# The head of a fused attention and expert kernel: key rows, query casts and the order of the first tiles

## The chip, the cores and the metric

The kernel runs on one core of one Trainium2 chip. The metric is the device time of one execution in microseconds (us); lower is better. TensorE is called PE, VectorE DVE, ScalarE ACT, GpSimd POOL and SyncE SP, as in the profile.

## The reference

Attention with pooled keys and values feeds a mixture of four experts:

```python
k_p = k.reshape(B, H, Sp, 8, D).mean(axis=3)        # B 8, H 8, S 576, D 64, Sp 72
v_p = v.reshape(B, H, Sp, 8, D).mean(axis=3)
attn = softmax(q @ k_p^T / sqrt(D))                 # 576 x 72 per head
x = (attn @ v_p) as (B*S, H*D)                      # 4608 x 512
p = domain_probs / (domain_probs.sum(-1) + 1e-9)
out = sum over e of p[:, e] * (relu(x @ w1[e]) @ w2[e])   # w1 512x1024, w2 1024x512, 4 experts
```

All inputs and the output are float32 in DRAM.

## The kernel before, in words

**Tiling.** The 4608 tokens are 36 tiles of 128 (`t`), four to a group of 512 (9 groups). For each tile the kernel makes the scores of 8 heads against 72 pooled keys (`scores`, line 381), subtracts the row maximum (`less_max`, 392), takes the exponential (`expo`, 405), turns the result (`turn_e`, 438) and multiplies with the pooled values (`context`, 458, or `context_turned`, 487). Queries have to be turned so that the head dimension lies on the partitions (`turn_q`, 352): for early tiles PE transposes rows of bf16 queries (`qrow`) into PSUM and ACT copies them out; for tiles from `DT` = 11 on DVE transposes 32x32 blocks of a block-wise loaded batch (`qblk`), with no work for PE. The experts are steps `s` (9 groups x 4 experts) of eight `up` products (503) and four `down` products (534), each of 128x512 outputs; `collect` (546) adds the weighted result and stores a tile after the last expert.

**Order.** The program is written out by hand (`manual_schedule`, 71): each engine executes its instructions in the order in which the code emits them. After the head, a loop over steps and slots (697) emits one `up` or `down` per slot and, from a plan with slots (571 to 611), the attention work of later tiles. A load by POOL converts float32 to bf16 on its way. It takes one of eight semaphores in turn, so each waits, on POOL, for the landing of the eighth before it.

**The loads at the start.** SP loads the first batch's keys as float32 in three parts (rows 0 to 1, 2 to 3, and the last 64 rows, 148), with the queries of tiles 0 and 1 (`q01`, float32, 512 KB) between the second part and the last (159 to 161). Then come the domain probabilities. POOL prepares masks, then waits in `after` (187, called in 191) for the second key part, by copying one element of it, and from there issues loads: values of batch 0, w1 of expert 0 with `q23` (queries of tiles 2 and 3 as bf16) between its halves, w2 of expert 0, and so on up to w2 of expert 3 and the queries of tile 9 (192 to 212).

**The head** (624 to 695) is a straight list. DVE folds the pooled keys (`fold`, 267; `last_k`, 275), PE transposes them (`turn_k`, 292), ACT casts the queries of tiles 0 and 1, and the first four tiles go through attention one after another, with the first expert's products for single tiles (`up_tile`, 515) between. `warm(n)` (615) issues n products of zeros on PE, of which nothing is used. The queries of tile 2 are turned in line 652, behind `context(0)` and `divide(0)`:

```python
    context(0)
    divide(0)
    turn_q(2)
    warm(5)
    turn_x(0, copy_v)
    turn_e(1)
    turn_q(3)
    scores(2)
```

Of the kernel before, what the change touches and what calls it, by code (L numbers as in the profile page):

```python
# [10 lines left out]
ALU = mybir.AluOpType  # L11
# [6 lines left out]
def kernel(  # L18
# [26 lines left out]
    ROWS = H * SP  # L45
    NB = 5
    TAIL = ROWS - (NB - 1) * P
    DT = 2 * TPG + 3
    EXP_SCALE = 1.0 / (float(D) ** 0.5 * POOL)
    NZ = 4  # L50
    BLK = 32
# [5 lines left out]
    raw = ctx.enter_context(tc.tile_pool(name="raw", bufs=1))  # L57
    prep = ctx.enter_context(tc.tile_pool(name="prep", bufs=2))
    qpool = ctx.enter_context(tc.tile_pool(name="qpool", bufs=8))
    qbpool = ctx.enter_context(tc.tile_pool(name="qbpool", bufs=2))  # L60
    soft = ctx.enter_context(tc.tile_pool(name="soft", bufs=2))
    grp = ctx.enter_context(tc.tile_pool(name="grp", bufs=2))
# [18 lines left out]
    def rows_of(src):  # L81
        return src.rearrange("h (j r) d -> (h j) (r d)", r=POOL)

    def load_rows(eng, dst, rows, parts=((0, NB - 1), (NB - 1, NB))):
        for i0, i1 in parts:
            if i1 == NB:
                src, to = rows[i0 * P:ROWS], dst[0:TAIL, i0, :]
            else:
                src = rows[i0 * P:i1 * P].rearrange("(i p) x -> p i x", p=P)
                to = dst[:, i0:i1, :]  # L90
            eng.dma_start(out=to, in_=src)  # L91

    def load_k(b):
        load_rows(nc.gpsimd, kraw[b % 2], rows_of(k[b]))
# [17 lines left out]
    def load_q(t):  # L112
        qrow[t] = qpool.tile([P, NPAIR, 2, D], BF16, name="qrow")
        for b, tok, n, at in segments(t * P, P):
            for z in range(2):
                nc.gpsimd.dma_start(
                    out=qrow[t][at:at + n, :, z, :],
                    in_=q[b][z * NPAIR:(z + 1) * NPAIR, tok:tok + n, :].rearrange(
                        "c p d -> p c d"
                    ),  # L120
                )
# [12 lines left out]
    def load_w1(e, halves=(0, 1)):  # L134
        for half in halves:
            cols = slice(half * (F // 2), (half + 1) * (F // 2))
            nc.gpsimd.dma_start(
                out=w1_sb[e][:, :, cols],
                in_=moe_w1[e].rearrange("(kc p) f -> p kc f", p=P)[:, :, cols],
            )  # L140
# [3 lines left out]
            out=w2_sb[e][:], in_=moe_w2[e].rearrange("(fb p) d -> p fb d", p=P)  # L144
        )


    KPARTS = ((0, 2), (2, NB - 1), (NB - 1, NB))
    k0 = raw.tile([P, NB, POOL * D], F32, name="k0")
    q01 = raw.tile([P, H, 2, D], F32, name="q01")  # L150
    q23 = raw.tile([P, H, 2, D], BF16, name="q23")

    def load_qg(eng, dst, c):
        eng.dma_start(
            out=dst[:],
            in_=q[0][:, 0:G, :].rearrange("h (p c) d -> p h c d", c=TPG)[:, :, c:c + 2],
        )

    load_rows(nc.sync, k0, rows_of(k[0]), KPARTS[:2])
    load_qg(nc.sync, q01, 0)  # L160
    load_rows(nc.sync, k0, rows_of(k[0]), KPARTS[2:])
    dp0 = const.tile([P, TPG, E], F32, name="dp0")
    nc.sync.dma_start(
        out=dp0[:], in_=moe_domain_probs[0:G].rearrange("(p c) e -> p c e", c=TPG)
# [22 lines left out]
    def after(landed):  # L187

        nc.gpsimd.tensor_copy(out=gate[:], in_=landed)

    after(k0[0:1, NB - 2, POOL * D - 1:POOL * D])
    load_v(0)
    load_w1(0, (0,))
    load_qg(nc.gpsimd, q23, 2)
    load_w1(0, (1,))
    load_w2(0)
    load_w1(1)
    ident32 = const.tile([NL, NL], F32, name="ident32")
# [10 lines left out]
    load_w1(3)  # L209
    load_q(TPG + 4)  # L210
    load_w2(3)
    load_q(TPG + 5)

    vblks = [raw.tile([P, NB, NZ, D], BF16, name=f"vblk{i}") for i in range(2)]
    nc.scalar.memzero(vraw[0][TAIL:P, NB - 1, :])
# [14 lines left out]
    mask_v = const.tile([P, NB, MZ, D], BF16, name="mask_v")  # L230

    def spread_mask():
        nc.vector.tensor_copy(
            out=mask_v[:], in_=own[:, :, 1:NZ].unsqueeze(3).to_broadcast([P, NB, MZ, D])
        )

# [30 lines left out]
    def fold(rows, i0, i1, *widths):  # L267
        for n in widths:
            w = n * D
            nc.vector.tensor_add(  # L270
                out=rows[:, i0:i1, 0:w], in0=rows[:, i0:i1, 0:w],
                in1=rows[:, i0:i1, w:2 * w],
            )

    def last_k(b, rows, i0, i1, n=P):

        if i0 == 0:
            pads[b] = prep.tile([P, NB, 2, D], BF16, name="kpad")
        shape = [n, i1 - i0, 2, D]
        nc.vector.tensor_add(  # L280
            out=pads[b][0:n, i0:i1],
            in0=rows[0:n, i0:i1, 0:D].unsqueeze(2).to_broadcast(shape),
            in1=rows[0:n, i0:i1, D:2 * D].unsqueeze(2).to_broadcast(shape),
        )
# [60 lines left out]
    def turned(dst, blocks, nm, copy=None):  # L345
        n = len(blocks)
        ps = ps_t.tile([P, n, P], BF16, tag="t", name=f"{nm}_ps")
        for i, block in enumerate(blocks):
            nc.tensor.transpose(ps[:, i, :], block, ident[:])  # L349
        (copy or nc.scalar.copy)(out=dst, in_=ps[:])  # L350

    def turn_q(t, copy=None):
        qT[t] = soft.tile([P, NPAIR, P], BF16, name="qT")
        if t >= DT:
            for b, tok, n, at in segments(t * P, P):
                nc.vector.transpose(  # L356
                    out=qT[t][:, :, at:at + n],
                    in_=qblk[b][:].rearrange("p (c a) j -> p c (a j)", c=NPAIR)[
                        :, :, tok:tok + n
                    ],  # L360
                )
            return
        if 2 <= t < TPG:
            ps = ps_t.tile([P, NPAIR, P], BF16, tag="t", name="qT_ps")
            for h in range(H):
                z, c = divmod(h, NPAIR)
                nc.tensor.transpose(
                    ps[z * D:(z + 1) * D, c, :], q23[:, h, t - 2, :], ident[:]
                )
            (copy or nc.scalar.copy)(out=qT[t][:], in_=ps[:])  # L370
            return
        if t < 2:
            qrow[t] = qpool.tile([P, NPAIR, 2, D], BF16, name="qrow")
            nc.scalar.copy(
                out=qrow[t][:],
                in_=q01[:, :, t, :].rearrange("p (z c) d -> p c z d", z=2),
            )
        flat = qrow[t][:].rearrange("p c z d -> p (c z d)")
        turned(qT[t][:], [flat[:, i * P:(i + 1) * P] for i in range(NPAIR)], "qT", copy)

    def scores(t):
        sc = ps_s.tile([P, 2, 512], F32, name="sc")
# [55 lines left out]
    def turn_e(t, copy=None):  # L438
        eT[t] = soft.tile([P, NB, P], BF16, name="eT")
        e = ebuf[t % 2]  # L440
        turned(eT[t][:], [e[:, i * P:(i + 1) * P] for i in range(NB)], "eT", copy)
# [14 lines left out]
    xps = {}  # L456

    def context(t):
        xps[t] = ps = ps_t.tile([P, DM], F32, tag="t", name="x_ps")
        for b, _, n, at in segments(t * P, P):  # L460
            for c, (i, z0, z1) in enumerate(CHUNKS):
                nc.tensor.matmul(  # L462
                    ps[at:at + n, (2 * i - 2 + z0) * D:(2 * i - 2 + z1) * D],
                    lhsT=eT[t][:, i, at:at + n],
                    rhs=vblk[b][:, i, z0:z1].rearrange("p z d -> p (z d)"),
                    start=(c == 0), stop=(c == NB - 1),
                )

    def divide(t):
        rows_x[t] = soft.tile([P, H, D], BF16, name="xr")  # L470
        nc.vector.tensor_tensor(
            out=rows_x[t][:], in0=xps.pop(t)[:].rearrange("p (h d) -> p h d", d=D),
            in1=es.pop(t)[:].unsqueeze(2).to_broadcast([P, H, D]), op=ALU.mult,
        )

    def x_columns(t):
        g, col = t // TPG, (t % TPG) * P
# [4 lines left out]
    def turn_x(t, copy=None):  # L482
        flat = rows_x.pop(t)[:].rearrange("p h d -> p (h d)")
        dst = x_columns(t)
        turned(dst, [flat[:, i * P:(i + 1) * P] for i in range(KC)], "xT", copy)

    def context_turned(t):
        ps = ps_t.tile([P, KC, P], F32, tag="t", name="xT_ps")
# [126 lines left out]
    def warm(n):  # L615

        ps = ps_h.tile([P, 2 * P], F32, tag="h", name="warm_ps")
        for _ in range(n):
            nc.tensor.matmul(ps[:], lhsT=zero[:, 0:P], rhs=zero[:])

    def copy_v(out, in_):
        nc.vector.tensor_copy(out=out, in_=in_)  # L622

    fold(k0, 0, 2, 4, 2)
    last_k(0, k0, 0, 2)
    fold(k0, 2, 4, 4, 2)
    last_k(0, k0, 2, 4)
    spread_mask()
    fold(k0[0:TAIL], 4, 5, 4, 2)
    last_k(0, k0, 4, 5, TAIL)  # L630
    warm(34)
    turn_k(0, copy_v, (
        lambda: None, lambda: None, lambda: None,
        lambda: (warm(12), turn_q(0), warm(2)),
    ))
    warm(3)
    scores(0)
    turn_q(1)
    less_max(0)
    expo(0)  # L640
    warm(10)
    scores(1)
    less_max(1)
    sum_v_by_products(0)
    turn_e(0)
    expo(1)
    spread_v(0)
    warm(5)
    sums_by_products(0)
    context(0)  # L650
    divide(0)
    turn_q(2)
    warm(5)
    turn_x(0, copy_v)
    turn_e(1)
    turn_q(3)
    scores(2)
    less_max(2)
# [3 lines left out]
    context(1)  # L662
    divide(1)
    turn_e(2)
    turn_x(1, copy_v)
    scores(3)
    less_max(3)
    up_tile(0, 1, (0,))
# [1 line left out]
    sums_by_products(2)  # L670
    context(2)
    divide(2)
    up_tile(0, 0, (1,))
    up_tile(0, 1, (1,))
    turn_x(2, copy_v)
    turn_e(3)
    domain_first()
    up_tile(0, 2, (0,))
# [10 lines left out]
    down(0, 2)  # L689
    collect(0, 2)  # L690
    load_k(2)
    load_v(2)
    load_q(TPG + 6)
    load_qblk(2)
    load_qblk(3)

    for s in range(NSTEP):
# [41 lines left out]
```

## Time and profile before

| what | us |
|---|---|
| median of 3 runs | 565.67 (565.13 to 566.07) |
| the profiled execution | 566.62 |
| its span, first to last instruction | 564.9 |
| PE busy, DVE, ACT, POOL | 553.8, 275.1, 251.9, 70.7 |
| granted clock of PE, mean | 0.999 |
| PE first at the turn of tile 2's queries | 17.61 |
| PE first at the dense products of step 1 (L509) | 37.51 |

The profile is of one execution. Its page gives the busy time of each engine, the span in 40 slices with the busy share of each in tenths, the transfer queues, the chain of work that ended last, and the costliest groups. Views of the trace give the instructions in order of time: start, duration, engine, line of the code, operation, output <- input, and in brackets how long the engine had been idle and what ended that. A line number is that of kernel.py and can be a helper's: L349 is the transpose in `turned`, whatever tile it works on. Matmuls overlap, so a group's duration is longer than its share of the chain.

### The profile page before, as it was taken

How to read it: one execution, taken by the hardware profiler on the slowest of the kernel's cores; microseconds unless marked ns; L12 is line 12 of the kernel's file. 1: busy time of each engine (PE TensorE's matmuls, PEld its weight loads, DVE VectorE, ACT ScalarE, POOL GpSimd, SP SyncE). 2: the span in 40 equal slices, each digit the busy share in tenths (PEclk: the TensorE clock that was granted, in tenths of full speed). 3: DMA queues.
4: the chain of work that ended last, by engine and by line, in shares of the span. 5: the costliest groups of instructions: out<-in, count | busy, mean ns of one | idle time of the engine just before them, and what ended most of it. 6: DMA issues, size and time to landing. Idle time of an engine off the chain costs nothing.

```text
span 564.9 us, 7779 instructions
## 1 busy us (share of the span) xinstructions
PE 553.8 (98%) x3259; PEld 278.9 (49%) x3259; DVE 275.1 (49%) x457; ACT 251.9 (45%) x434; POOL 70.7 (13%) x95
## 2 busy tenths in 40 slices
PE   6899999999999999999999999999999999999996
PEld 5764555444444444444444444444444444444443
DVE  4655745444564445644555444654456444422222
ACT  4645645444544444544454444444454444433330
POOL 6245460000220001300050003000000000000000
PEclk9999999999999999999999999999999999999999
DMA  8999998200390011900192017301000100001001
GB/s 198 203 201 197 200 136 169 42 1 1 77 125 0 2 38 39 116 9 20 57 84 43 1 75 31 12 1 57 19 1 2 38 37 0 2 37 38 1 0 75
DMA packets 88723, 33.67 MB, mean 60 GB/s; under 512 B 65616, under 2 KB 83472, under 8 KB 88688
## 3 DMA queue, kind: packets, MB, share of 16 engines
q0 software_dynamic: 81648, 21.96, 40.2%
q1 hardware_dynamic: 7040, 11.22, 5.5%
q8 instruction: 25, 0.41, 0.3%
q14 instruction: 10, 0.08, 0.0%
HBM read 45.69 MB, written 9.44 MB: 98 GB/s over the span
## 4 chain that ended last, share of the span: by engine, by line
PE 95%; DVE 2%; DMA 1%; ACT 0%; issue 0%; SPq 0%; ACTq 0%
PE o_ps L541 44%; PE h_ps L509 42%; PE xT_ps L492 3%; PE sc L385 2%; PE eT_ps L349 2%; DMA k<-in_k_dram 1%; PE h_ps L524 1%; PE kT_ps L298 0%; PE qT_ps L349 0%; DVE mx L396 0%; DVE d_sb L398 0%; DVE kraw L270 0%; DVE xT L622 0%; PE x_ps L462 0%; PE v_ps L334 0%
## 5 line engine op out<-in xcount | busy, mean ns | idle before, releaser
L509 PE MATMUL h_ps<-xT,w 128*128 128x512 bf16 x1120 | 274.5, 379 | 0.0
L541 PE MATMUL o_ps<-w,h_sb 128*128 128x512 bf16 x1152 | 271.5, 379 | 0.0
L513 ACT ACTIVATE h_sb<-h_ps 128x512 bf16<-128x512 f32 x280 | 167.1, 597 | 228.5 <-PE h_ps L509 228.2
L541 PEld LDWEIGHTS <-h_sb 128*128 128x128 bf16 x1152 | 112.3, 98 | 133.6
L556 DVE SCALAR_TENSOR_TENSOR acc<-o_ps,p_sb,acc 128x512 f32<-128x512 f32 x108 | 81.0, 750 | 191.0 <-PE o_ps L541 190.6
L509 PEld LDWEIGHTS <-w 128*128 128x128 bf16 x1120 | 105.3, 98 | 110.4
L552 DVE TENSOR_SCALAR acc<-o_ps,p_sb 128x512 f32<-128x512 f32 x36 | 27.0, 750 | 68.0 <-PE o_ps L541 67.9
L497 ACT CAST xT<-xT_ps 128x512 bf16<-128x512 f32 x32 | 18.7, 586 | 46.9 <-PE xT_ps L492 46.9
L128 POOL DMA_DIRECT2D qblk<-in_q_dram x24 | 26.8, 1129 | 55.4 <-DVE qT L356 54.3
L396 DVE TENSOR_REDUCE mx<-sc 128x8 f32<-128x576 f32 x36 | 27.2, 755 | 10.4 <-PE sc L385 10.4
L91 POOL DMA_DIRECT2D kraw<-in_k_dram x14 | 9.2, 664 | 167.4 <-DVE kpad L280 166.3
L398 DVE TENSOR_TENSOR d_sb<-sc,mx 128x576 f32<-128x576 f32 x36 | 27.3, 757 | 1.4
L350 ACT COPY eT<-eT_ps 128x640 bf16<-128x640 bf16 x36 | 24.7, 687 | 2.6 <-PE eT_ps L349 2.6
L433 DVE TENSOR_TENSOR ebuf<-e_sb,rs 128x576 bf16<-128x576 f32 x32 | 24.2, 757 | 1.1
L431 DVE TENSOR_REDUCE total<-e_sb 128x8 f32<-128x576 f32 x32 | 23.8, 744 | 1.4 <-ACT e_sb L412 1.4
L412 ACT ACTIVATE e_sb<-d_sb 128x576 f32<-128x576 f32 x32 | 21.9, 684 | 4.5 <-DVE d_sb L398 1.9
L492 PEld LDWEIGHTS <-vblk 128*128 128x128 bf16 x288 | 17.3, 98 | 7.5
L492 PE MATMUL xT_ps<-eT,vblk 128*128 128x128 bf16 (+1 forms) x288 | 19.6, 213 | 0.0
L356 DVE STREAM_TRANSPOSE qT<-qblk 128x512 bf16<-128x512 bf16 (+1 forms) x28 | 17.7, 641 | 0.0
L349 PEld LDWEIGHTS <-ebuf 128*128 128x128 bf16 x180 | 12.9, 98 | 8.9 <-ACT ebuf L412 1.2
L349 PE MATMUL eT_ps<-ident,ebuf 128*128 128x128 bf16 x180 | 15.9, 219 | 1.0 <-ACT ebuf L412 1.0
L385 PE MATMUL sc<-kT,qT 128*128 128x144 bf16 (+1 forms) x160 | 15.0, 227 | 0.9 <-DVE kT L622 0.5
(74 smaller groups left out, 188.5 us busy)
## 6 DMA issues: line engine op xcount, KB each, us to landing
out_dram<-acc SPq DMA_DIRECT2D x36, 256.0 KB, 2.0
vraw<-in_v_dram POOLq DMA_DIRECT2D x8, 512.0 KB, 6.1
w<-in_moe_w_dram POOLq DMA_DIRECT2D x8, 512.0 KB, 11.1
w<-in_moe_w_dram POOLq DMA_DIRECT2D x4, 1024.0 KB, 15.5
kraw<-in_k_dram POOLq DMA_DIRECT2D x7, 512.0 KB, 6.3
qblk<-in_q_dram POOLq DMA_DIRECT2D x24, 144.0 KB, 6.7
k<-in_k_dram SPq DMA_DIRECT2D x2, 512.0 KB, 3.8
qrow<-in_q_dram POOLq DMA_DIRECT2D x12, 64.0 KB, 10.5
```

What stands on the lines that cost most here:

```text
L128: nc.gpsimd.dma_start(out=qblk[b][n32 * BLK:(n32 + 1) * BLK], in_=q[b][z * NPAIR:(z + 1) * NPAIR, :, half * BLK:(half + 1) * BLK] .rearran ...
L349: nc.tensor.transpose(ps[:, i, :], block, ident[:])
L350: (copy or nc.scalar.copy)(out=dst, in_=ps[:])
L385: nc.tensor.matmul(sc[at:at + n, pair // 2, (pair % 2) * PW:(pair % 2 + 1) * PW], lhsT=qT[t][:, pair, at:at + n], rhs=kT[b][:, pair * PW:( ...
L396: nc.vector.reduce_max(out=mx[:], in_=view, axis=AX.X)
L398: nc.vector.tensor_tensor(out=ds[t][:], in0=view, in1=mx[:].unsqueeze(3).to_broadcast([P, 2, 4, SP]), op=ALU.subtract,)
L492: nc.tensor.matmul(ps[:, pair, at:at + n], lhsT=vblk[b][:, i, z0:z0 + 2].rearrange("p z d -> p (z d)"), rhs=eT[t][:, i, at:at + n], start= ...
L509: nc.tensor.matmul(ps[:], lhsT=w1_sb[e][:, kc, fb * P:(fb + 1) * P], rhs=xT[g][:, kc, :], start=(kc == 0), stop=(kc == KC - 1),)
L513: nc.scalar.activation(out=hs[s][:, fb, :], in_=ps[:], func=ACT.Relu)
L541: nc.tensor.matmul(ps[:], lhsT=hs[s][:, fb, i * P:(i + 1) * P], rhs=w2_sb[e][:, fb, :], start=(fb == 0), stop=(fb == FB - 1),)
L552: nc.vector.tensor_scalar_mul(out=accs[t][:], in0=ps[:], scalar1=p_sb[:, e, t:t + 1])
L556: nc.vector.scalar_tensor_tensor(out=accs[t][:], in0=ps[:], scalar=p_sb[:, e, t:t + 1], in1=accs[t][:], op0=ALU.mult, op1=ALU.add,)
```

## The change

It rewrites the start of the program and moves two tiles between two ways of turning:

- SP loads all three key parts first and the queries of tiles 0 and 1 behind them. The last 64 key rows are summed by POOL in three adds instead of by DVE.
- POOL's `after` waits for the first key part instead of the second. POOL's loads then start with the values, the three adds, and w1 of expert 0.
- Queries of tiles 2 and 3 are no longer a bf16 load by POOL. `load_qg(2)` loads them as float32 on SP into the one buffer that tiles 0 and 1 had, after these are cast, and `cast_q` casts each on POOL.
- The cast of tile 0, the copies of its turned queries and turned context, and its division are each split into two halves, for two engines or in two instructions. The mask is spread by ACT instead of DVE.
- `context` takes its PSUM from the other pool. The warm-up products are put elsewhere and in other numbers; `turn_x(0)` comes behind `turn_e(1)`, and `up_tile(0, 0, (1,))` ahead of `scores(3)`.
- `DT` is 9 instead of 11: DVE turns the queries of tiles 9 and 10, and their row loads are gone. The block load of batch 2 comes ahead of that batch's values.

```diff
-    DT = 2 * TPG + 3
+    DT = 2 * TPG + 1
...
+    load_rows(nc.sync, k0, rows_of(k[0]), KPARTS)
+    qg = {}
+    def load_qg(c):
+        tile2 = qgpool.tile([P, H, 2, D], F32, name="qg")
+        nc.sync.dma_start(
+            out=tile2[:],
             in_=q[0][:, 0:G, :].rearrange("h (p c) d -> p h c d", c=TPG)[:, :, c:c + 2],
         )
-    load_rows(nc.sync, k0, rows_of(k[0]), KPARTS[:2])
-    load_qg(nc.sync, q01, 0)
-    load_rows(nc.sync, k0, rows_of(k[0]), KPARTS[2:])
+        qg[c], qg[c + 1] = tile2[:, :, 0, :], tile2[:, :, 1, :]
+    load_qg(0)
...
-    after(k0[0:1, NB - 2, POOL * D - 1:POOL * D])
+    after(k0[0:1, 1, POOL * D - 1:POOL * D])
     load_v(0)
-    load_w1(0, (0,))
-    load_qg(nc.gpsimd, q23, 2)
-    load_w1(0, (1,))
+    nb = NB - 1
+    for w in (4 * D, 2 * D, D):
+        nc.gpsimd.tensor_add(
+            out=k0[0:TAIL, nb, 0:w], in0=k0[0:TAIL, nb, 0:w], in1=k0[0:TAIL, nb, w:2 * w]
+        )
+    load_w1(0)
     load_w2(0)
...
     load_w2(3)
-    load_q(TPG + 5)
...
+    def cast_q(t, *parts):
+        qrow[t] = qpool.tile([P, NPAIR, 2, D], BF16, name="qrow")
+        for copy, c0, c1 in parts:
+            copy(
+                out=qrow[t][:, c0:c1],
+                in_=qg[t].rearrange("p (z c) d -> p c z d", z=2)[:, c0:c1],
+            )
...
+    turn_k(0, dve, (lambda: None, lambda: warm(11)))
+    cast_q(0, (act, 0, 2), (dve, 2, NPAIR))
+    warm(7)
+    turn_q(0)
+    cast_q(1, (act, 0, NPAIR))
     warm(3)
     scores(0)
     turn_q(1)
     less_max(0)
     expo(0)
-    warm(10)
+    load_qg(2)
+    warm(12)
     scores(1)
...
     context(0)
-    divide(0)
+    for t in (2, 3):
+        cast_q(t, (nc.gpsimd.tensor_copy, 0, NPAIR))
+    divide(0, ((0, 4), (4, H)))
     turn_q(2)
-    warm(5)
-    turn_x(0, copy_v)
-    turn_e(1)
+    turn_e(1, dve)
+    turn_x(0)
     turn_q(3)
     scores(2)
...
-    turn_x(1, copy_v)
+    turn_x(1, dve)
+    up_tile(0, 0, (1,))
     scores(3)
...
     load_k(2)
+    load_qblk(2)
     load_v(2)
-    load_q(TPG + 6)
-    load_qblk(2)
     load_qblk(3)
```

More of the change, by code (lines that the diff above doesn't have):

```diff
@@ L59 @@
     qpool = ctx.enter_context(tc.tile_pool(name="qpool", bufs=8))
+    qgpool = ctx.enter_context(tc.tile_pool(name="qgpool", bufs=1))
     qbpool = ctx.enter_context(tc.tile_pool(name="qbpool", bufs=2))
@@ L149 @@
     k0 = raw.tile([P, NB, POOL * D], F32, name="k0")
[L150 to L155, printed above, removed]
+    load_rows(nc.sync, k0, rows_of(k[0]), KPARTS)
[4 more added lines that the diff above has]
+            out=tile2[:],
             in_=q[0][:, 0:G, :].rearrange("h (p c) d -> p h c d", c=TPG)[:, :, c:c + 2],
         )
-    load_rows(nc.sync, k0, rows_of(k[0]), KPARTS[:2])
-    load_qg(nc.sync, q01, 0)
-    load_rows(nc.sync, k0, rows_of(k[0]), KPARTS[2:])
+        qg[c], qg[c + 1] = tile2[:, :, 0, :], tile2[:, :, 1, :]
+    load_qg(0)
     dp0 = const.tile([P, TPG, E], F32, name="dp0")
@@ L232, in spread_mask @@
     def spread_mask():
-        nc.vector.tensor_copy(
+        nc.scalar.copy(
             out=mask_v[:], in_=own[:, :, 1:NZ].unsqueeze(3).to_broadcast([P, NB, MZ, D])
@@ L350, in turned, with turned_by_halves @@
         (copy or nc.scalar.copy)(out=dst, in_=ps[:])
+    def turned_by_halves(dst, blocks, nm):
+        m = len(blocks) // 2
+        turned(dst[:, 0:m, :], blocks[:m], nm)
+        turned(dst[:, m:, :], blocks[m:], nm, nc.vector.tensor_copy)
+    def cast_q(t, *parts):
[5 more added lines that the diff above has]
+            )
     def turn_q(t, copy=None):
@@ L362, in turn_q @@
             return
[L363 to L377, printed above, removed]
-        flat = qrow[t][:].rearrange("p c z d -> p (c z d)")
-        turned(qT[t][:], [flat[:, i * P:(i + 1) * P] for i in range(NPAIR)], "qT", copy)
+        flat = qrow[t][:].rearrange("p c z d -> p (c z d)")
+        blocks = [flat[:, i * P:(i + 1) * P] for i in range(NPAIR)]
+        if t == 0:
+            turned_by_halves(qT[t][:], blocks, "qT")
+        else:
+            turned(qT[t][:], blocks, "qT", copy)
     def scores(t):
@@ L458, in context @@
     def context(t):
-        xps[t] = ps = ps_t.tile([P, DM], F32, tag="t", name="x_ps")
+        xps[t] = ps = ps_o.tile([P, DM], F32, tag="o", name="x_ps")
         for b, _, n, at in segments(t * P, P):
@@ L467, in context, with divide @@
                 )
-    def divide(t):
+    def divide(t, parts=((0, H),)):
         rows_x[t] = soft.tile([P, H, D], BF16, name="xr")
[L471 to L474, printed above, removed]
+        ps, rs = xps.pop(t)[:].rearrange("p (h d) -> p h d", d=D), es.pop(t)
+        for h0, h1 in parts:
+            nc.vector.tensor_tensor(
+                out=rows_x[t][:, h0:h1], in0=ps[:, h0:h1],
+                in1=rs[:, h0:h1].unsqueeze(2).to_broadcast([P, h1 - h0, D]), op=ALU.mult,
+            )
     def x_columns(t):
@@ L484, in turn_x @@
         dst = x_columns(t)
-        turned(dst, [flat[:, i * P:(i + 1) * P] for i in range(KC)], "xT", copy)
+        blocks = [flat[:, i * P:(i + 1) * P] for i in range(KC)]
+        if t == 0:
+            turned_by_halves(dst, blocks, "xT")
+        else:
+            turned(dst, blocks, "xT", copy)
     def context_turned(t):
@@ L619, in warm @@
             nc.tensor.matmul(ps[:], lhsT=zero[:, 0:P], rhs=zero[:])
-    def copy_v(out, in_):
-        nc.vector.tensor_copy(out=out, in_=in_)
+    act, dve = nc.scalar.copy, nc.vector.tensor_copy
+    spread_mask()
     fold(k0, 0, 2, 4, 2)
     last_k(0, k0, 0, 2)
+    warm(28)
     fold(k0, 2, 4, 4, 2)
     last_k(0, k0, 2, 4)
[L628 to L635, printed above, removed]
+    nc.vector.tensor_copy(
+        out=pads[0][0:TAIL, NB - 1],
+        in_=k0[0:TAIL, NB - 1, 0:D].unsqueeze(1).to_broadcast([TAIL, 2, D]),
+    )
+    turn_k(0, dve, (lambda: None, lambda: warm(11)))
[3 more added lines that the diff above has]
+    cast_q(1, (act, 0, NPAIR))
     warm(3)
@@ L645 @@
     turn_e(0)
+    spread_v(0)
     expo(1)
-    spread_v(0)
-    warm(5)
+    warm(7)
     sums_by_products(0)
     context(0)
-    divide(0)
+    for t in (2, 3):
+        cast_q(t, (nc.gpsimd.tensor_copy, 0, NPAIR))
+    divide(0, ((0, 4), (4, H)))
     turn_q(2)
-    warm(5)
-    turn_x(0, copy_v)
-    turn_e(1)
+    turn_e(1, dve)
+    turn_x(0)
     turn_q(3)
@@ L672 @@
     divide(2)
-    up_tile(0, 0, (1,))
     up_tile(0, 1, (1,))
-    turn_x(2, copy_v)
+    turn_x(2, dve)
     turn_e(3)
```

## The prediction

> **What bounds the kernel now.** I read the page first: engine shares, then the 40 slices.
>
> ```profile
> span 564.9 us, 7779 instructions
> PE 553.8 (98%) x3259; PEld 278.9 (49%) x3259; DVE 275.1 (49%) x457; ACT 251.9 (45%) x434; POOL 70.7 (13%) x95
> ...
> DMA  8999998200390011900192017301000100001001
> ```
>
> TensorE (PE) is busy 98% of the span, and asked for waits after 50 us, the trace names none for PE: from there on the time is PE's own work, and a change gains only by taking PE work away. Everything else is the head. The DMA row says something more: the transfers are full for the first 95 us or so, although PE hardly waits for them.
>
> Second view, POOL's instructions in order of time. POOL (GpSimd) issues all converting loads itself:
>
> ```profile
> 5.67 0.71 POOL L189 COPY gate<-k 1x1 f32<-1x1 f32 x1 [3.64 <-DMA k<-in_k_dram]
> 6.32 1.45 POOL L91 DMA_DIRECT2D vraw<-in_v_dram  x2
> 7.74 0.81 POOL L137 DMA_DIRECT2D w<-in_moe_w_dram  x1
> 8.52 0.93 POOL L154 DMA_DIRECT2D q<-in_q_dram  x1
> ...
> 47.88 1.48 POOL L137 DMA_DIRECT2D w<-in_moe_w_dram  x2 [1.79 <-DMA w<-in_moe_w_dram]
> 49.35 1.50 POOL L116 DMA_DIRECT2D qrow<-in_q_dram  x2
> 50.82 0.93 POOL L143 DMA_DIRECT2D w<-in_moe_w_dram  x1
> 54.76 1.50 POOL L116 DMA_DIRECT2D qrow<-in_q_dram  x2 [3.02 <-DMA w<-in_moe_w_dram]
> ```
>
> POOL does one thing after another. The 1x1 copy that gates the loads waits for the keys, and the loads stand behind it until it is done. Later the loads themselves wait: each converting load waits for the landing of the eighth one before it, so POOL is held in its own queue until 51.75 us (50.82 + 0.93), when it has issued w2 of expert 3.
>
> Third view, PE around 17 us:
>
> ```profile
> 17.13 0.55 PE L462 MATMUL x_ps<-vblk,eT 128*128 128x128 bf16 x5
> 17.61 0.42 PE L367 MATMUL qT_ps<-ident,q 128*64 128x128 bf16 x8
> 17.96 0.72 PE L619 MATMUL warm_ps<-zero 128*128 128x256 bf16 x5
> ```
>
> Behind the context of tile 0, PE turns the queries of tile 2 (17.61), from q23, which POOL's load of 8.52 brought as bf16.
>
> **The change, part by part.** The order of instructions in the built program decides it. In the changed kernel tiles 2 and 3 no longer come by a converting load. `load_qg(2)` loads them as f32 on SP, and `cast_q` for t = 2, 3 converts them on POOL. The program writes these casts after all of the loads up to `load_w2(3)`, so on POOL they are the two instructions right after that load:
>
> ```
> 44 DMACopy    w2 of expert 3 <- dram   (waits for an earlier load)
> 45 TensorCopy qrow(2) <- qg            (waits for SP's load)
> 46 TensorCopy qrow(3) <- qg
> 47 DMACopy    kraw (batch 2) <- dram
> ```
>
> PE's first weight load of `turn_q(2)` waits for POOL, row 45. Behind it in PE's queue stands everything else: turn_e(1), turn_x(0), scores(2), all up and down products. So PE stands still from some 17 us until POOL has passed row 44. There is no deadlock: POOL's loads wait only for earlier loads.
>
> When does POOL pass row 44? Today at 51.75. What moves it:
> - q23 leaves the stream of converting loads. POOL is woken by the landings: first half of w1(0) at 16.26, second half, with q23 between, at 20.93, so 4.67 us; later halves alone take 2.54 (25.99 to 28.53) and 2.57. q23 thus costs 2.1: **-2.1**.
> - SP's `load_qg(2)`, 512 KB of f32, goes beside that stream. The keys moved at 379 GB/s between 3 and 5 us, which makes 1.4 us; at the converting stream's 205 GB/s it would be 2.5, and 0 if it fits beside it. **+1.4** (0 to 2.5): it goes by the keys' queue.
> - The gate opens with the first key part (DVE is released by it at 4.13) instead of the second (5.67): up to 1.5 earlier. Against that, three adds on 64 rows, which wait for the last key rows, now stand on POOL ahead of w1(0). POOL has no such row; its nearest, a 128x128 select, took 0.29, its 1x1 copy 0.71. Three make 0.9 to 2.1 and the wait is unknown, but v0's 576 KB (2.8 us at 205 GB/s) cover most. **-0.7** (-1.5 to +1.0).
>
> Sum 51.75 - 1.4 = 50.35 (48.15 to 53.15). On SP, `load_qg(2)` waits for the casts of tiles 0 and 1; behind it stand only the output's stores, the first at 84.9. On POOL the next loads (keys and values of batch 2, blocks of queries) stand behind the casts; the keys are first folded at 86.7 today, and PE will be 34 us later still. Two loads of queries fewer (tiles 9 and 10) stand behind that point and do not count.
>
> The cast of 128x512 from f32 on POOL is not in the trace. ACT's took 0.62; four times POOL's 128x128 select is 1.16, twice that 2.3. I take **1.1** (0.6 to 2.3), nearest to the select. The second cast runs while PE and ACT work on tile 2. With 0.05 for the signal, PE goes on at 51.5 instead of 17.6: **+33.9**.
>
> By the Trainium skill, "GPSIMD Engine Reference", section 3.1, a tight one-input loop over 512 elements takes 0.77 us; the sum would be 0.3 lower. No row here shows it.
>
> What hides behind that stall, and so counts nothing now: the last key rows ahead of the queries, their adds on POOL, the mask on ACT, the halves of casts, copies and division for tiles 0 and 1, x_ps in the other PSUM pool, fewer warm-up products ahead of `turn_q(2)`. They move PE's arrival at the wait from 17.6 to perhaps 16, and PE waits that much longer. Without the stall they would be the gain (rival 1).
>
> What stands behind the stall and counts:
> - The rest of the head, 17.6 to 37.3, runs again in the same order of dependences. The chain there goes scores(2), maximum, difference, exponential, turn_e(2): DVE 0.76 + 0.76 and ACT 0.68, unchanged. The five warm products at 17.96 (0.65 on the chain) go; turn_x(0) now follows turn_e(1), and up_tile(0, 0, (1,)) moves ahead of scores(3), so tile 3's scores start later while PE idles less. **-0.3** (-1.0 to +0.5).
> - Tiles 9 and 10 are turned by DVE. PE loses twice four transposes of 0.22 on the chain (such a group is shown below): **-0.45**. DVE pays twice 0.70 (its transposes at 122.5 and 137.3), beside PE; it is busy 49%, and tile 9's scores come some 2.8 us after the turn (78.27 to 81.08). The block of queries must have landed; with PE 34 us late it has.
>
> ```profile
> 44.89 0.22 PE qT_ps L349 x4
> ```
>
> - PE comes out of an idle of 34 us. At the program's start, busy time of PE by windows, all warm-up products of one shape:
>
> ```profile
> 2.00:4.00 2.00, 2.00 (x12) 1.44 (x11) 0.00 (x0) 1.98 (x7) 0.03 (x1) 1.00 0.94 342
> 4.00:6.00 2.00, 2.00 (x21) 1.79 (x19) 1.80 (x4) 0.91 (x5) 0.33 (x1) 1.00 0.81 265
> ```
>
> (columns: window, length, PE busy and count, weight loads, DVE, ACT, POOL, granted clock, DMA share, GB/s.) Twelve products in the first 2 us, 21 in the next, at a granted clock that the column gives as 1.00 in both: PE starts at about half pace, whatever that column says, and gets to full pace near 4 us. 34 products took 5.19 us and would have taken 3.6 at the later pace of 0.107, so the start cost about 1.5. After the stall PE is thinly used at first, and part of that hides in waits for DVE and ACT: **+1.2** (0 to 3.9, rival 2).
>
> Sum: 33.9 - 0.3 - 0.45 + 1.2 = +34.35. The profiled execution took 566.62 (span 564.9 and 1.7 around it): 566.62 + 34.35 = 600.97. It stands 0.95 over the median of the runs, 565.67, which I take off: **600.0 us**.
>
> **The rivals.**
> 1. The casts come in time (the change does what it says; this is the faster side). That needs POOL's arithmetic to pass loads that wait. The price: the chain now runs from the last key rows (transfer done 10.02) to the first scores (12.24). With those rows ahead, the queries are last at about 9.6; half a cast (0.35), transposes (0.4), half a copy (0.35) and three signals put the scores at 10.85: -1.4. With -0.45 for the turns and -0.65 for the warm products it gives 563.2. For it: nothing in the trace. Against it: the gate of 5.67, which does its work only because loads stay behind POOL's copy, and the order in which all POOL rows appear. It decides if the casts run before about 17 us: 4%.
> 2. PE stays at half pace through the rest of the head, until the dense products. For it: the head is transposes and short groups, with PE busy 4.88 of 6.40 us between 17.6 and 24. The chain's PE rows there (0.35, 0.29, 0.42, 0.37, 0.45, 0.29) would double, +2.2, and as at the start a further 1.7 would be lost in the first 3.4 us of dense work: +3.9 in place of +1.2, 602.7. Against: the groups of 16 products begin already at 20.1. 20%. The Trainium skill, "TensorE: Matmul & The Clock Gate", Part 4 (PE-mode transpose), says that transposes don't count as activity for the clock; by that rule this rival is the likely one. No row of this case separates it, since the warm-up products always stand between.
> 3. The converting stream gets a good deal faster or slower, because SP's load and POOL's adds land differently than I price them: 48.15 or 53.15 instead of 50.35, 597.8 or 602.8. Inside the range.
>
> **How the numbers follow.** Forecast (stall to about 51 us, clock soon back) 74%, rival 2 20%, rival 1 4%, a stall of quite another length 2%. The steps' ends around 600.0: stream -2.2/+2.8, cast -0.5/+1.2, clock -1.2/+2.7, rest of the head -0.7/+0.8; they are independent, and as roots of summed squares give -2.7/+4.2. Range 597 to 604.5; it holds rivals 2 and 3. What a measurement of this kernel can tell from no change is about 0.2%, 1.1 us. Faster by more: rival 1 alone, 0.04. Same: 0.01 (casts late by a few us). Slower: 0.95.
>
> **What would show it.** Right: POOL's first cast of qrow from qg between 49 and 53 us, right behind the issue of the last w2 load; one idle of PE of 33 to 35 us ahead of qT_ps, put down to POOL; the slices of PE at 0 from the second to the fourth; the loop after it at the same pace; no PE qT_ps for tiles 9 and 10, two more DVE transposes. The cast's row decides the 1.1, POOL's last wait the 50.35, the spacing of the first products after the stall the clock. Wrong: a cast of qrow on POOL before 20 us, or PE at work between 20 and 45 us.

## The result and the profile after

The changed kernel takes 601.91 us (601.5 to 602.29) against 565.48 for the kernel before on the same chip (medians of four runs each); the ratio is 1.0639, 95% interval 1.0626 to 1.0652. The forecast was 600.0, range 597 to 604.5.

The page of the changed kernel, the rows that answer to those of before:

```profile
span 600.6 us, 7742 instructions
PE 557.0 (93%) x3240; PEld 281.0 (47%) x3240; DVE 276.3 (46%) x460; ACT 251.0 (42%) x433; POOL 69.4 (12%) x95
...
PE   9004999999999999999999999999999999999997
...
PEclk9655999999999999999999999999999999999999
DMA  9999992042009600193019201900100010001001
```

PE's busy time is nearly what it was (557.0 against 553.8); what is new are two empty slices, of 15 us each, and parts of their neighbours. The granted clock (PEclk, in tenths) falls in these slices too. The transfers go on at 9 tenths through them and the other engines' work is small, so PE seems to wait for something that stands late in a queue. POOL's instructions in order of time name it:

```profile
47.98 1.48 POOL L138 DMA_DIRECT2D w<-in_moe_w_dram  x2 [1.80 <-DMA w<-in_moe_w_dram]
49.44 1.50 POOL L117 DMA_DIRECT2D qrow<-in_q_dram  x2
50.91 0.92 POOL L144 DMA_DIRECT2D w<-in_moe_w_dram  x1
51.78 1.21 POOL L364 CAST qrow<-qg 128x512 bf16<-128x512 f32 x2
```

The casts of tiles 2 and 3 (L364) come directly behind the last w2 load, as the order of the program says, and PE goes on when the first of them is done (L353 is the transpose in `turned`):

```profile
52.50 0.61 PE L353 MATMUL qT_ps<-ident,qrow 128*128 128x128 bf16 x4 [36.27 <-POOL qrow L364]
```

The bracket holds the stall: 36.27 us of idle PE, ended by POOL's write of qrow. From 73 us to the end the list of PE's waits has one row of 0.3 us.

Where the 35.7 us between the two profiled spans (600.6 - 564.9) lie:

| stretch | before | after | difference |
|---|---|---|---|
| start to PE's turn of tile 2's queries | 17.61 | 52.50 | +34.89 |
| from there to the first dense product | 19.90 | 21.37 | +1.47 |
| from there to the end | 527.39 | 526.73 | -0.66 |

The first dense products, before and after:

```profile
37.51 5.34 PE L509 MATMUL h_ps<-xT,w 128*128 128x512 bf16 x24
...
73.87 5.34 PE L521 MATMUL h_ps<-xT,w 128*128 128x512 bf16 x24
```

### The profile page after: what moved, and what is told of

The parts are those of the page before. It is cut to its first block, busy times and chain, and to the rows that moved or that the text cites. A ratio compares the mean times of both kernels' runs of the same rounds, so it can differ in the third digit from the quotient of the medians.

```text
span 600.6 us, 7742 instructions
## 1 busy us (share of the span) xinstructions
PE 557.0 (93%) x3240; PEld 281.0 (47%) x3240; DVE 276.3 (46%) x460; ACT 251.0 (42%) x433; POOL 69.4 (12%) x95
## 4 chain that ended last, share of the span: by engine, by line
PE 89%; DMA 6%; POOL 2%; DVE 1%; issue 1%; ACT 0%; SPq 0%; DVEq 0%; POOLq 0%; ACTq 0%
PE o_ps L553 41%; PE h_ps L521 40%; DMA w<-in_moe_w_dram 6%; PE xT_ps L504 2%; PE eT_ps L353 2%; PE sc L391 2%; PE h_ps L536 1%; DMA k<-in_k_dram 1%; POOL w L138 1%; PE qT_ps L353 0%; PE kT_ps L302 0%; POOL w L144 0%; POOL k L197 0%; PE xT_ps L353 0%; DVE kraw L274 0%
## 5 line engine op out<-in xcount | busy, mean ns | idle before, releaser
L353 PE MATMUL qT_ps<-ident,qrow 128*128 128x128 bf16 x36 | 4.1, 239 | 36.4 <-POOL qrow L364 36.3
L354 ACT COPY qT<-qT_ps 128x512 bf16<-128x512 bf16 (+1 forms) x9 | 5.0, 559 | 40.4 <-PE qT_ps L353 40.4
L353 PEld LDWEIGHTS <-qrow 128*128 128x128 bf16 x36 | 2.8, 106 | 38.5 <-POOL qrow L364 36.5
L373 DVE STREAM_TRANSPOSE qT<-qblk 128x512 bf16<-128x512 bf16 (+1 forms) x30 | 19.1, 645 | 0.0
```

## The experiments

Theory: the casts are late because of their place in POOL's queue, behind loads that wait. Rivals: the queries themselves come late (the load, not the cast); POOL is the wrong engine for the casts; the 1.47 is the new order and not the clock. Each kernel was timed beside the kernel before, whose medians there were 566.00 (first four) and 566.06 (last four). "Turn" is PE's start of tile 2's turn, "dense" the first dense product, both from the profile.

| kernel | turn | dense | span | median | ratio to before (95%) |
|---|---|---|---|---|---|
| changed | 52.50 | 73.87 | 600.6 | 601.91 | 1.0639 (1.0626 to 1.0652) |
| casts on ACT and DVE | 25.16 | 46.34 | 572.9 | 573.91 | 1.0140 (1.0125 to 1.0155) |
| casts early on POOL | 16.08 | 36.07 | 562.7 | 564.59 | 0.9974 (0.9965 to 0.9984) |
| casts midway on POOL | 38.54 | 59.90 | 586.3 | 587.75 | 1.0384 (1.0368 to 1.0399) |
| stall filled | 52.25 | 72.25 | 599.0 | 600.07 | 1.0604 (1.0588 to 1.0620) |
| before, DVE turns 9 and 10 | 16.76 | 36.61 | 563.5 | 565.98 | 0.9993 (0.9985 to 1.0002) |
| changed, q23 as before | 16.34 | 36.53 | 563.6 | 565.74 | 0.9992 (0.9983 to 1.0001) |
| early casts, no halves | 16.44 | 36.03 | 562.5 | 564.14 | 0.9964 (0.9951 to 0.9977) |
| before, keys first | 17.29 | 37.14 | 564.2 | 566.15 | 1.0006 (0.9997 to 1.0015) |

### The casts on other engines

```diff
-    for t in (2, 3):
-        cast_q(t, (nc.gpsimd.tensor_copy, 0, NPAIR))
+    cast_q(2, (act, 0, NPAIR))
+    cast_q(3, (dve, 0, NPAIR))
```

> Casts of tiles 2 and 3 on ACT and DVE instead of POOL; the load of their queries stays where the change put it. Theory (the stall is the place of the casts in POOL's queue): PE no longer waits for POOL but for the load itself, which SP issued at 11.11 and which landed 13.1 later in the changed kernel, at 24.2; with a cast of 0.62 PE goes on at about 24.9 instead of 52.5, so 601.9 - 27.6 = 574.3 us, with a granted clock that still falls. Rival (the transfers as a whole hold PE up, wherever the cast is done): 600 to 602 us. Second rival (the casts were all that was wrong): about 563.5 us.

28 of the 36 us go, and 8 stay. In its timeline the next wait shows itself:

```profile
24.48 0.62 ACT L364 CAST qrow<-qg 128x512 bf16<-128x512 f32 x1 [8.21 <-DMA qg<-in_q_dram]
...
25.16 0.61 PE L353 MATMUL qT_ps<-ident,qrow 128*128 128x128 bf16 x4 [8.73 <-ACT qrow L364]
```

ACT idles 8.21 us for the load `qg`, which SP could issue only at about 11, when tiles 0 and 1 had been cast out of the one buffer. Behind the wait for POOL stood a wait for the transfer; the first had covered it.

### The casts early in POOL's queue, with the load early too

```diff
-    qgpool = ctx.enter_context(tc.tile_pool(name="qgpool", bufs=1))
+    qgpool = ctx.enter_context(tc.tile_pool(name="qgpool", bufs=2))
     load_qg(0)
+    load_qg(2)
...
     make_identity(nc, ident32[:])
+    for t in (2, 3):
+        qrow[t] = qpool.tile([P, NPAIR, 2, D], BF16, name="qrow")
+        nc.gpsimd.tensor_copy(
+            out=qrow[t][:], in_=qg[t].rearrange("p (z c) d -> p c z d", z=2)
+        )
     load_k(1)
...
-    load_qg(2)
-    for t in (2, 3):
-        cast_q(t, (nc.gpsimd.tensor_copy, 0, NPAIR))
```

> The same two casts on the same POOL, but ahead of its first load that waits; the queries of tiles 2 and 3 get a buffer of their own and are loaded on SP right behind those of tiles 0 and 1. Theory (place in the queue): POOL casts at about 12.6 to 13.9, PE is not held at the turn of tile 2 at 16.2, no loss of clock, 563 to 564.5 us. Rival (POOL is too slow for casts, or a cast and the descriptors of its loads hinder each other): a wait for POOL of several us stays, over 567 us.

The same instruction on the same engine, at another place in its queue:

```profile
12.66 1.16 POOL L208 CAST qrow<-qg 128x512 bf16<-128x512 f32 x2
13.77 1.31 POOL L92 DMA_DIRECT2D kraw<-in_k_dram  x2
...
16.08 0.39 PE L359 MATMUL qT_ps<-ident,qrow 128*128 128x128 bf16 x4
```

PE does not wait at the turn (16.08 has no bracket). The kernel is 0.26% faster than the one before (interval 0.16 to 0.35%): POOL was not the wrong engine. This run moves the load and the casts at once; the next one keeps the early load and moves the casts alone.

### The casts midway

Against the kernel with early casts:

```diff
     make_identity(nc, ident32[:])
-    for t in (2, 3):
...
     load_k(1)
...
     load_w1(2)
+    for t in (2, 3):
+        qrow[t] = qpool.tile([P, NPAIR, 2, D], BF16, name="qrow")
+        nc.gpsimd.tensor_copy(
+            out=qrow[t][:], in_=qg[t].rearrange("p (z c) d -> p c z d", z=2)
+        )
```

> As the one before, but with the casts behind the second half of w1 of expert 2 in POOL's queue, which the changed kernel issued by 39.86. Theory (the stall is as long as the part of the queue ahead of the casts): PE goes on at 39 to 40.5 instead of 52.5, 588.5 to 590 us. Rival (the stall ends when the loads have all landed or the queries have come, whatever the place): 563 to 565, or 600 to 602 us.

```profile
37.12 0.74 POOL L138 DMA_DIRECT2D w<-in_moe_w_dram  x1 [4.10 <-DMA w<-in_moe_w_dram]
37.86 1.17 POOL L213 CAST qrow<-qg 128x512 bf16<-128x512 f32 x2
...
38.54 0.61 PE L359 MATMUL qT_ps<-ident,qrow 128*128 128x128 bf16 x4 [22.43 <-POOL qrow L213]
...
38.97 1.48 POOL L117 DMA_DIRECT2D qrow<-in_q_dram  x2
```

PE goes on at 38.54, 0.7 behind the start of the cast, as in the changed kernel (51.78 and 52.50). The queries had landed long before. POOL was done with the load ahead of the casts (w1 of expert 2) at 39.86 in the changed kernel and at 37.86 here, since the stream ran ahead without a load of SP in its midst; so the time is 0.75 us under the expected range. With the casts at 12.66, 37.86 and 51.78 PE stood still for 0, 22.43 and 36.27 us: the stall follows the place.

### The stall filled with products of zeros

```diff
+    warm(320)
     turn_q(2)
     turn_e(1, dve)
```

> The changed kernel with 320 products of zeros on PE ahead of the turn of tile 2, which fill the stall (320 x 0.107 = 34 us); they compute nothing that is used. Theory (the 1.5 us more from the turn of tile 2 to the first dense product, 21.37 against 19.90, are the lower clock after the idle time): the granted clock stays at 1.0, PE goes on at 52.5 as before, and the time falls by 1.5 us to about 600.4. Rival (those 1.5 us are the new order of the head): 601.9 us.

The time came as expected. The turn and the first dense product:

```profile
52.25 0.40 PE L353 MATMUL qT_ps<-ident,qrow 128*128 128x128 bf16 x4 [1.14 <-POOL qrow L364]
...
72.25 5.34 PE L521 MATMUL h_ps<-xT,w 128*128 128x512 bf16 x24
```

From turn to dense: 20.00 here, 21.37 in the changed kernel, 19.90 before. So 1.37 of the 1.47 is the clock, and 0.10 the new order; the two other kernels whose PE stood still took 21.18 (casts on ACT and DVE) and 21.36 (midway). The windows of the changed kernel (columns as in the prediction) show the granted clock while PE is idle, after it starts again, and at its return:

```profile
50.00:52.50 2.50, 0.00 (x0) 0.00 (x1) 0.00 (x0) 0.00 (x0) 2.50 (x5) 0.50 1.25 206
52.50:57.50 5.00, 4.72 (x44) 4.23 (x45) 2.30 (x4) 1.56 (x4) 2.86 (x4) 0.50 1.44 198
58.00:58.50 0.50, 0.32 (x3) 0.00 (x0) 0.14 (x1) 0.50 (x2) 0.29 (x1) 0.79 1.31 194
58.50:59.00 0.50, 0.30 (x5) 0.28 (x5) 0.50 (x1) 0.15 (x1) 0.50 (x1) 1.00 1.95 170
```

and of the kernel with the stall filled, at 1.00 throughout:

```profile
18.00:50.00 32.00, 32.00 (x296) 28.67 (x294) 0.00 (x0) 0.00 (x0) 12.26 (x18) 1.00 1.33 203
52.00:58.00 6.00, 3.96 (x61) 3.43 (x62) 3.34 (x8) 3.12 (x6) 3.26 (x6) 1.00 1.41 198
```

### Single parts

Before, with the turns of tiles 9 and 10 on DVE alone:

```diff
-    DT = 2 * TPG + 3
+    DT = 2 * TPG + 1
...
-    load_q(TPG + 5)
...
-    load_v(2)
-    load_q(TPG + 6)
     load_qblk(2)
+    load_v(2)
```

> The kernel before with one part of the change alone: DVE turns tiles 9 and 10, their row loads are gone, the block load of batch 2 comes ahead of its values. Theory: PE loses eight transposes of 0.22 per four and nothing else changes, -0.45 us; what lay behind the first dense product was shorter by 0.66 in the changed kernel, so between -0.4 and -0.7 us. Rival (DVE's transposes delay its other work, or the block load comes late): 0 or slower.

The time does not resolve it: the ratio makes -0.4 us, its interval -0.85 to +0.1. The earlier turn of 16.76 is not the edit's: the head is the same up to there, and its first transfers land up to 1 us apart from one execution to another (first scores at 11.17 here, 12.24 in the profile of before). The spans behind the first dense product say more: 527.39 and 527.06 in the two kernels with PE's turns, 526.40 to 527.07, mean 526.69, in the eight with DVE's. That is -0.54, with a spread of 0.3 to 0.4 to either side; the lowest of the one sort and the highest of the other meet (527.06 and 527.07), so the gain is likely and not shown.

The changed kernel with q23 as a converting load again, and `turn_q` reading it as before:

```diff
-    load_w1(0)
+    load_w1(0, (0,))
+    q23 = raw.tile([P, H, 2, D], BF16, name="q23")
+    nc.gpsimd.dma_start(
+        out=q23[:],
+        in_=q[0][:, 0:G, :].rearrange("h (p c) d -> p h c d", c=TPG)[:, :, 2:4],
+    )
+    load_w1(0, (1,))
...
-    load_qg(2)
...
-    for t in (2, 3):
-        cast_q(t, (nc.gpsimd.tensor_copy, 0, NPAIR))
```

> The changed kernel with one part undone: the queries of tiles 2 and 3 come again as a converting load by POOL between the halves of w1 of expert 0, and there is no cast on POOL. Theory (all the loss comes from the casts' place, and what is left is worth little because the next wait is near): the stall goes; PE then waits for that load, which lands behind the first half of w1 (15.8 in the changed kernel) by 2.1, at about 17.9 against 16.1 when nothing holds it, so about 1.8 us over the kernel with early casts, 565.8 to 566.5 us. Rival (the rest of the change costs or gains several us by itself): below 564 or over 568 us.

The time fell just under the expected range, but not by the expected way: the turn came at 16.34 and not at 17.9, so q23 had landed by then and held PE hardly longer than the early casts (16.08). The loss is gone with the casts, as the theory needs. The rest of the change is then worth little by itself: the ratio to before has 0.9983 to 1.0001 as its interval.

The kernel with early casts, with no halves:

```diff
-            turned_by_halves(qT[t][:], blocks, "qT")
+            turned(qT[t][:], blocks, "qT")
...
-            turned_by_halves(dst, blocks, "xT")
+            turned(dst, blocks, "xT", nc.vector.tensor_copy)
...
-    cast_q(0, (act, 0, 2), (dve, 2, NPAIR))
+    cast_q(0, (act, 0, NPAIR))
...
-    divide(0, ((0, 4), (4, H)))
+    divide(0)
```

> The kernel with early casts on POOL, with the halves undone: the cast, the copies of turned queries and turned context and the division of tile 0 each in one instruction on one engine. Theory (halves shorten the chain to the first scores by a half cast and a half copy): first scores 0.4 later, and 0.3 to 0.6 us slower than the kernel with early casts. Rival (the two engines hinder each other, or something else is late anyway): the same or faster.

The first scores come 0.56 later (11.16 against 10.60), the turn of tile 2 0.36 (16.44 against 16.08), and the dense products at 36.03 against 36.07: the halves' gain is gone before it reaches the end. It is gone already at tile 3's turn (17.89 against 17.93), behind tile 0's turned context, whose four transposes span 0.38 in one piece and 0.66 in halves. My theory was wrong there; this is the fastest kernel of the study, by no margin that the two sets of runs could tell from the one with halves.

Before, with the last key rows ahead of the queries and nothing else:

```diff
-    load_rows(nc.sync, k0, rows_of(k[0]), KPARTS[:2])
+    load_rows(nc.sync, k0, rows_of(k[0]), KPARTS)
     load_qg(nc.sync, q01, 0)
-    load_rows(nc.sync, k0, rows_of(k[0]), KPARTS[2:])
```

> The kernel before with one part of the change alone: SP loads the last key rows ahead of the queries; DVE still folds them. Theory (the queries of tiles 2 and 3 land at 17.6 and hold PE there whatever comes earlier): first scores at about 11.5 instead of 12.24, but the turn of tile 2 stays at about 17.6 and the time within 0.3 us of before. Rival (the first scores' delay is carried to the end): 0.8 us faster.

```profile
10.52 0.41 PE L384 MATMUL sc<-kT,qT 128*128 128x144 bf16 x4 [0.50 <-DVE kT L621]
...
17.29 0.42 PE L366 MATMUL qT_ps<-ident,q 128*64 128x128 bf16 x8 [1.19 <-DMA q<-in_q_dram]
```

The first scores come 0.65 to 1.72 earlier than in the two profiles with the old order (11.17 and 12.24), and PE then waits 1.19 for q23: the time is that of before. By that wait this part can pay only together with an earlier way for the queries of tile 2, as the kernel with early casts has it; no run adds the two alone.

## Why the prediction was right, and where its sizes were not

- **The order decides: right.** Casts behind the issue of the last w2 load, one long wait of PE for POOL, empty slices, two DVE transposes more (30 against 28): as named. The idle was 36.27 and not 33 to 35, and two slices are empty and not three: PE came to the wait at 16.23, where the sum counts from 17.6 though the prediction itself says "perhaps 16". Three places in the queue gave no stall, a middle one and the full one.
- **When POOL passes row 44: 50.35 forecast, 51.78 measured**, the same as before the change (51.75). So the -1.4 that I summed up did not come. The end of the last w2 load's issue in all ten profiles tells the terms apart, though kernels alike up to there differ by up to 0.6:

| start of the loads | queries of tiles 2 and 3 | end of that issue |
|---|---|---|
| old | q23 by POOL | 51.75, 51.14, 51.70 |
| new | q23 by POOL | 50.19 |
| new | early by SP | 50.32, 49.84, 50.21 |
| new | late by SP | 51.83, 51.44, 51.57 |

  The new start gave about 1.3 where I had 0.7, and the late load cost about 1.5, near my 1.4. The failed term is q23's 2.1: with its queries on SP early instead, POOL was no sooner. What q23 takes in the transfers when nothing comes in its place, no run shows.

  SP's late load, issued at 11.11, took 13.1 us to land, and while it went the converting stream slowed: w2 of expert 0 landed at 26.09, 6.5 behind the second half of w1(0) (19.55), where it was 5.1 before. With the load early it landed at 24.16:

```profile
26.09 0.61 POOL L117 DMA_DIRECT2D qrow<-in_q_dram  x1 [5.92 <-DMA w<-in_moe_w_dram]
...
24.16 0.61 POOL L117 DMA_DIRECT2D qrow<-in_q_dram  x1 [4.31 <-DMA w<-in_moe_w_dram]
```

- **The cast: 1.1 forecast, 0.66 measured** (0.60 when early). Taking four times POOL's 128x128 select was the wrong row; ACT's cast of the same shape, 0.62, was near. The Trainium skill's 0.77 ("GPSIMD Engine Reference", section 3.1) is nearer than my choice and also above the trace.
- These two make 52.50 instead of 51.5, +1.0 of the 1.35 us by which the sum (+34.35 against +35.70 in the spans) was short. Part of that nearness is luck: the cast was 0.44 cheaper and the new start gained 0.6 more than I had, and that hid part of q23's 2.1. The other 0.57 between 600.0 and 601.91 is the profiled executions, which stood 0.95 over the median before and 0.38 after.
- **The rest of the head: -0.3 forecast, +0.10 measured** (stall filled against before). The five products of zeros, priced at 0.65 on the chain, gave only 0.16: tile 2's exponential was turned 4.91 us behind the turn of tile 2's queries (57.16 - 52.25) instead of 5.07 (22.68 - 17.61), since PE now waited there for ACT's copies (0.45 and 0.33). The scores of tile 3, now behind `up_tile(0, 0, (1,))`, came 6.37 behind instead of 5.63, and the gain was gone.
- **The clock: +1.2 forecast, +1.37 measured.** Rival 2 (low until the dense loop, +3.9) fell: the clock came back at 58.2, 5.7 us after PE's restart, well ahead of 73.87. Its rule, that transposes don't count as activity (the Trainium skill, "TensorE: Matmul & The Clock Gate", Part 4), is not borne out as I applied it. With the casts on ACT and DVE, PE restarted at 25.16, its first products that are no transposes began at 27.70, and the clock rose in this window, at about 29.84:

```profile
29.00:30.00 1.00, 1.00 (x16) 1.00 (x14) 0.94 (x2) 0.00 (x0) 0.00 (x0) 0.58 1.23 206
30.00:30.50 0.50, 0.50 (x11) 0.31 (x7) 0.29 (x2) 0.43 (x1) 0.00 (x0) 1.00 1.25 209
```

  So 2.1 us of other products were enough there; in the changed kernel it took 3.2 and with the casts midway 3.8. The Trainium skill, same page, Part 1, asks for some 3.4 us of sustained activity. What exactly is counted stays open.
- **The turns on DVE: -0.45 forecast**, about -0.54 by the spans, which overlap; by the time alone not resolved.
- **Rival 1, the change doing what it says: 563.2, that is 2.5 under before; 1.4 measured** (interval 0.9 to 2.0) when the casts come early. Its first scores were right (10.85 forecast, 10.68 measured), but its -0.65 for the products of zeros failed as above, and it named one condition where there are two: the load must come earlier as well, or the time is 573.91.

## What to carry to other kernels

An instruction on a queue that also issues waiting transfers costs little by its own length, 0.66 us here, and much by all that stands ahead of it, 36 us here: look up what the last instruction before it waits for, and when. When a wait of that size is taken away, ask what it had covered; here the load of the same data, 8 us, was the next one. The best repair tried was neither another engine nor less work but the same two instructions earlier in the program, with a second buffer for their load.

## What the runs showed of the hardware

- A 512 KB float32 load on SP landed 12.6 to 13.2 us after its issue at 11 us, beside POOL's converting stream, and 5.7 to 6.9 us after it at the program's start.
- The granted clock fell to 0.50 some 3.2, 4.4 and 4.9 us after PE stopped (casts on ACT and DVE, changed kernel, casts midway), and came back 4.7, 5.7 and 6.4 us after its restart. At the program's start the column shows 1.00 while PE does 12 products of zeros in 2 us and then 21 (before), so it can't be read there.
- One cast of 128x512 from float32 to bf16 took 0.43 on DVE, 0.62 on ACT and 0.60 to 0.66 on POOL; POOL's adds of 64x256, 64x128 and 64x64 float32 took 0.88, 0.52 and 0.31.
